# Masked attention followed by an ELU layer: the two products six blocks behind attention, the weight conversion over three engines, the first batch loaded in long pieces

## The chip, the cores and the metric

The kernel runs on one core of a Trainium2 chip, in one launch. The metric is the device time of one execution in microseconds (us); less is better. The time before is the median of three runs, 1208.84 us (1207.19 to 1209.16).

PE is TensorE (PEld its weight loads), ACT ScalarE, DVE VectorE, POOL GpSimd, and SP the engine on whose queue every DMA here is issued (SPq).

## What is computed

The input has 4 batches, 8 heads, 768 tokens and 64 numbers per head. Queries and keys are assigned to one of 16 cluster centroids per head, and a query attends only to keys of its own cluster. The heads are put side by side (512 numbers per token), and two products with an ELU between them follow. `w_in` and `w_out` arrive as 64-bit floats; all else is fp32.

```python
mask = q_assign[:, :, :, None] == k_assign[:, :, None, :]
scores = scale * np.matmul(q, k.transpose(0, 1, 3, 2))
scores = np.where(mask, scores, -1000000000.0)
attn = np.exp(scores - max); attn = attn / (sum(attn) + 1e-9)
x = (attn @ v) with heads side by side        # 3072 x 512
h = x @ w_in                                  # 512 -> 2048
out = where(h > 0, h, exp(min(h, 0)) - 1) @ w_out   # 2048 -> 512
```

## The kernel before

**Blocks.** Two heads make a pair, four pairs a batch, and the 768 queries of a pair are cut into two halves of 384. A pair and a half make a *block*: 8 blocks in a batch, 32 in all, in the order batch, pair, half.

**Attention of a block.** `score` (line 300) does six key tiles. For each, PE multiplies keys by queries for both heads (line 308, fp32, two heads side by side in the array) and adds the mask as a bf16 product of one-hot keys `hot` with `qm` (line 317); ACT takes the exponential into `p` (line 325). `add` (line 328) sums the six `p` for the denominator, on POOL in batch 0 and on DVE afterwards. `values` (line 337) multiplies by `v` into `o_bank`; `divide` (line 350) sums over the keys on PE (line 355), ACT copies that sum out (line 360), DVE takes its reciprocal (line 361), and POOL multiplies the output `xT` by it and keeps a running sum (lines 363 and 364).

**What a batch needs first.** `turn` transposes queries and keys of a pair on PE (line 232; a copy by ACT for queries, by DVE for keys). `similar` multiplies all four pairs by the centroids (line 249) and turns the result by halves on DVE (line 256); `assign` makes the one-hot tile `hot` (lines 263 to 274), `masks` the tile `qm` (line 280). `prepare` gives these steps for the next batch their places beside the current one. Queries and keys are loaded so that both heads of a token lie together, in packets of 256 bytes, two DMAs to a tile.

**The products.** `mlp` (line 367) makes four groups for each half of a batch: two of `hidden` (lines 375 to 388: 16 fp32 products into a bank, exponential on ACT, a clamp on POOL, the ELU's end on DVE one step later) and two of `outer` (lines 401 to 411, into `o_bank` or `f_bank`, then a copy and a DMA out). The groups of batch b run beside the attention of batch b+1, one group after each block. So batch 0 has attention alone, batches 1 to 3 both, and a last pass the eight groups of batch 3 alone.

**Weights.** 32 pieces (16 of `w_in`, then 16 of `w_out`) of 128 x 512 64-bit numbers, 512 KB each, are loaded as pairs of words and made fp32. `convert` (line 176) does this with six instructions on DVE (lines 187 to 199) and two on POOL (lines 188 and 200), each piece in two steps; words have two buffers. `weigh(2)` after every key tile of batch 0 takes two steps from this list. So all conversion lies in the opening and in batch 0.

**What sets the order.** Each engine does its instructions in the order in which the program writes them, and an instruction that waits holds up all behind it on that engine; the DMAs wait on SP in the same way. The score tiles, sums, transposes and hidden products share three PSUM tiles (`banks`) in turn.

Of the kernel before, what the change touches and what calls it, by code (L numbers as in the profile page):

```python
# [9 lines left out]
F32 = mybir.dt.float32  # L10
BF16 = mybir.dt.bfloat16
# [49 lines left out]
def main_path(ctx, tc, c, q, k, v, centroids, moe_w_in, moe_w_out, out):  # L61
# [19 lines left out]
    xtp = ctx.enter_context(tc.tile_pool(name="xtp", bufs=10))  # L81
# [12 lines left out]

    pairs = [(b, pr) for b in range(B) for pr in range(NPR)]
    raw = {}

    def load(name, i):
        b, pr = pairs[i]
        src = {"q": q, "k": k, "v": v}[name]  # L100
        if name == "v":
            t = raw[name, i] = loads.tile([P, 2, NT, D], F32, name="v_raw", tag=name, bufs=2)
# [4 lines left out]
            return  # L107
        t = loads.tile([P, NT, 2, D], F32, name=f"{name}_raw", tag=name, bufs=2)
        for e in range(2):
            nc.sync.dma_start(t[:, :, e], src[b, 2 * pr + e].rearrange("(p t) d -> p t d", t=NT))  # L110
        raw[name, i] = t.rearrange("p t h d -> p t (h d)")
# [3 lines left out]
    for name in "qk":  # L115
        load(name, 0)
    for name in "qk":
        load(name, 1)
# [53 lines left out]

    w_in, w_out = c["w_in"], c["w_out"]
    WC = 512
    wide = moe_w_in.dtype != F32

    def convert(to, src):

        if not wide:
            return [lambda: nc.sync.dma_start(to, src)]  # L180
        words = loads.tile([P, WC, 2], U32, name="words", tag="words", bufs=2)
        ex = loads.tile([P, WC], U32, name="ex", tag="ex", bufs=1)
        low, high, bits = words[:, :, 0], words[:, :, 1], to.bitcast(U32)
        nc.sync.dma_start(words.rearrange("p n w -> p (n w)"), src.bitcast(U32))

        def begin():
            nc.vector.tensor_scalar(bits, high, 0xFFFFF, None, op0=Alu.bitwise_and)
            nc.gpsimd.tensor_scalar(to, bits, 2.0**-20, 1.0, op0=Alu.mult, op1=Alu.add)
            nc.vector.tensor_scalar(  # L189
                ex, high, 20, 0x7FF, op0=Alu.logical_shift_right, op1=Alu.bitwise_and  # L190
            )
            nc.vector.tensor_scalar(ex, ex, -896.0, 0.0, op0=Alu.add, op1=Alu.max)  # L192
            nc.vector.tensor_scalar(ex, ex, 255.0, 2.0**23, op0=Alu.min, op1=Alu.mult)  # L193
            nc.vector.scalar_tensor_tensor(
                ex, high, 0x80000000, ex, op0=Alu.bitwise_and, op1=Alu.bitwise_or
            )

        def end():
            nc.vector.scalar_tensor_tensor(to, low, 2.0**-52, to, op0=Alu.mult, op1=Alu.add)
            nc.gpsimd.tensor_tensor(to, to, ex.bitcast(F32), op=Alu.mult)  # L200

        return [begin, end]

    def weights():
        for g in range(DF // WC):
            for ch in range(KC):
                yield w_in[:, ch, ts(g, WC)], moe_w_in[ts(ch, P), ts(g, WC)]
        for f in range(FC):
            yield w_out[:, f], moe_w_out[ts(f, P)]

    def weight_steps():

        held = None
        for to, src in weights():
            steps = convert(to, src)
            if held:
                yield from held
            held = steps
            yield lambda: None
        yield from held  # L220
# [7 lines left out]
    def turn(i, j):  # L228
        T[i, j] = turned.tile([P, S], F32, name=f"{name_of[j]}T", tag="turned")
        ps = banks()  # L230
        for t in range(NT):
            nc.tensor.transpose(ps[:, t // HT, ts(t % HT, P)], raw[name_of[j], i][:, t], ident)  # L232
        to = T[i, j].rearrange("p (h s) -> p h s", h=2)
        if j == 0:
            nc.scalar.copy(to, ps[:, :, :HS])
        else:
            nc.vector.tensor_copy(to, ps[:, :, :HS])  # L237

    def similar(b, j):
        sim[b, j] = route.tile([P, S], F32, name="sim", tag="sim", bufs=1)  # L240
        ps = banks()
        for half in range(2):
            cols = slice(half * HS, (half + 1) * HS)
            for x in range(2):
                for e in range(2):
                    for g in range(2):
# [5 lines left out]
                            rhs=T[b * NPR + pr, j][:, cols],  # L252
# [3 lines left out]
            nc.vector.transpose(sim[b, j][:, cols], ps[:, half, :HS])  # L256
# [19 lines left out]
    def masks(i):  # L276
        b, pr = pairs[i]
        qm[i] = route.tile([P, S], BF16, name="qm", tag="qm", bufs=2)
        s = big[:, pr : pr + 1]
        nc.vector.tensor_scalar(qm[i], hot[b, 0], s, s, op0=Alu.mult, op1=Alu.subtract)  # L280

    def prepare(b):

        plan = {}
        for pr in range(NPR):
            i = b * NPR + pr
            at = 2 * NT * pr
            for j in range(2):
                plan.setdefault(at + j, []).append(lambda i=i, j=j: turn(i, j))
            if i + 2 < len(pairs):  # L290
                plan[at + 1].append(lambda i=i: (load("q", i + 2), load("k", i + 2)))
        for j in range(2):
            plan.setdefault(6 * NPR * 2 - 10 + 2 * j, []).append(lambda j=j: similar(b, j))
            plan.setdefault(6 * NPR * 2 - 9 + 2 * j, []).append(lambda j=j: assign(b, j))
        plan.setdefault(6 * NPR * 2 - 4, []).append(lambda: masks(b * NPR))
        return plan


    pu, osum, xT = {}, {}, {}

    def score(i, half, kts):
        b, pr = pairs[i]
        cols = slice(half * HS, (half + 1) * HS)
        for kt in kts:
# [10 lines left out]
            for e in range(2):  # L315
# [4 lines left out]
                    rhs=qm[i][rows, cols],  # L320
# [3 lines left out]
            p = pu[i, half, kt] = probs.tile([P, 2, HS], F32, name="p", tag="p")  # L324
            nc.scalar.activation(p, s[:, :, :HS], Act.Exp, scale=SCALE)  # L325

    def add(i, half, kt, eng):
        if kt == 0:
            return
        if kt == 1:  # L330
            osum[i, half] = work.tile([P, 2, HS], F32, name="psum", tag="psum")
        to = osum[i, half]
        eng.tensor_tensor(  # L333
            to, pu[i, half, 0] if kt == 1 else to, pu[i, half, kt], op=Alu.add
        )

    def values(i, half, kt):
        for e in range(2):
            nc.tensor.matmul(  # L339
                o_bank[64 * e : 64 * e + 64, :HS],  # L340
                lhsT=raw["v", i][:, e, kt],
                rhs=pu[i, half, kt][:, e],
                start=(kt == 0),
                stop=(kt == NT - 1),
            )
        if kt == NT - 1:
            x = xT[i, half] = xtp.tile([P, HS], F32, name="xT", tag="xT")
            nc.scalar.copy(x, o_bank[:, :HS])
            divide(i, half)

    def divide(i, half):
        s = osum.pop((i, half))
# [6 lines left out]
        n = 2 * i + half  # L359
        nc.scalar.activation(r, d[:, :HS], Act.Copy, accum_out=d_sum[:, n : n + 1])  # L360
        nc.vector.reciprocal(r, r)  # L361
        x = xT[i, half]
# [4 lines left out]
    def mlp(b, half, last):  # L367
# [51 lines left out]
        for parts in (  # L419
            [(0, 0), (0, 1), (0, 2), (0, 3), (1, 0), (1, 1)],  # L420
# [6 lines left out]


    load("v", 0)
    rest = weight_steps()  # L430

    def weigh(n):
        for _ in range(n):
            step = next(rest, None)
            if step:
                step()

    plan = prepare(0)
    weigh(2)
    for n in sorted(plan):  # L440
        for step in plan[n]:
            step()
        weigh(1)

    units = 2 * NPR * NT
    pending = []

    def flush(left):
        while len(pending) > left:
            values(*pending.pop(0))  # L450

    for b in range(B + 1):
        groups = []
        if b > 0:
            for half in range(2):
                groups.extend(mlp(b - 1, half, b == B))
        plan = prepare(b + 1) if b + 1 < B else {}
        G = NT if b else 1
        assert b == 0 or len(groups) == units // G
        for n in range(0, units, G):  # L460
            if b:
                flush(0)
            if b < B:
                i, half, kt = b * NPR + n // (2 * NT), (n // NT) % 2, n % NT
                kts = range(kt, kt + G)
                within = range(n % (2 * NT), n % (2 * NT) + G)
                if 3 in within and i + 1 < len(pairs):
                    load("v", i + 1)
                score(i, half, kts)
                pending.extend((i, half, x) for x in kts)  # L470
                if 2 * NT - 3 in within and pairs[i][1] + 1 < NPR:
                    masks(i + 1)
                for x in kts:
                    add(i, half, x, nc.vector if b else nc.gpsimd)
            if b == 0:
                flush(2)
                weigh(2)
# [254 lines left out]
```

## Time and profile before

| | |
|---|---|
| median of three runs | 1208.84 us |
| the profiled execution | 1209.18 us |
| its span, first to last instruction | 1207.4 us |
| PE busy | 1078.6 us (89%) |
| DVE / POOL / ACT busy | 499.6 / 284.9 / 268.4 us |
| moved by DMA | 42.7 MB |

The median and the profiled execution differ by 0.34 us. The table's busy times are sums over the whole span; the stages differ much, so the sections below go by stage. Where a row has a granted clock, 1.00 is TensorE at 2.4 GHz all the time, and less means that it ran at 1.2 GHz for a part.

### The profile page before, as it was taken

The numbers are of one execution on the slowest core, as the hardware profiler recorded it, in microseconds if no ns is written. First come the engines' busy times: TensorE is split into PE (matmuls) and PEld (weight loads), VectorE is DVE, ScalarE is ACT, GpSimd is POOL, SyncE is SP. The second block draws the span as 40 slices with busy tenths as digits, with TensorE's granted clock in tenths as the row PEclk, the third lists the DMA queues.
The fourth block names the chain that finished last, engine by engine and source line by source line (L and its number), as shares of the span: only waits on it lengthen the run. The fifth ranks groups of instructions, "written<-read, shape, count | busy, mean of one in ns | idle before, by whom it ended". The sixth has DMA issues, their size and how long they took to land.

```text
span 1207.4 us, 10470 instructions
## 1 busy us (share of the span) xinstructions
PE 1078.6 (89%) x4291; PEld 522.1 (43%) x4291; DVE 499.6 (41%) x516; ACT 268.4 (22%) x395; POOL 284.9 (24%) x239
## 2 busy tenths in 40 slices
PE   5646374388999999999999999999999999999997
PEld 3212121125544555345544554455445544554553
DVE  5788888743432343523422344334323432110110
ACT  1112121122322232223322221223222322110100
POOL 2366666652210121112200111112101111110100
PEclk9778777789999999999999999999999999999999
DMA  9424232300001101001010000000000000000000
GB/s 231 119 70 110 71 110 73 103 1 26 14 24 31 38 14 40 10 31 27 14 35 30 1 14 10 9 23 1 22 10 22 1 10 9 9 0 18 9 9 20
DMA packets 62791, 42.73 MB, mean 35 GB/s; under 512 B 51472, under 2 KB 55568, under 8 KB 62736
## 3 DMA queue, kind: packets, MB, share of 16 engines
q1 hardware_dynamic: 62736, 41.98, 12.6%
q8 instruction: 36, 0.59, 0.2%
q14 instruction: 19, 0.16, 0.0%
HBM read 35.68 MB, written 6.29 MB: 35 GB/s over the span
## 4 chain that ended last, share of the span: by engine, by line
PE 79%; DVE 8%; POOL 7%; issue 3%; DMA 1%; SPq 1%; ACT 0%; POOLq 0%; ACTq 0%
PE banks L375 28%; PE o_bank L401 18%; PE f_bank L401 9%; PE banks L308 9%; PE o_bank L339 9%; POOL psum L333 3%; PE banks L317 2%; PE banks L249 2%; DVE ex L189 2%; POOL w_out L200 1%; PE banks L355 1%; DVE ex L193 1%; DVE r L361 1%; PE banks L232 1%; DVE ex L192 1%
## 5 line engine op out<-in xcount | busy, mean ns | idle before, releaser
L375 PE MATMUL banks<-xT,w_in 128*128 128x384 f32 x1024 | 334.6, 488 | 0.0
L375 PEld LDWEIGHTS banks<-xT,w_in 128*128 128x128 f32 x1024 | 193.5, 190 | 137.4 <-issue 5.9
L401 PE MATMUL o_bank<-w_out,gT 128*128 128x512 f32 x512 | 224.9, 595 | 0.0
L325 ACT ACTIVATE p<-banks 128x768 f32<-128x768 f32 x192 | 153.9, 810 | 148.5 <-PE banks L317 142.4
L361 DVE RECIPROCAL r<-r 128x384 f32<-128x384 f32 x32 | 81.7, 2552 | 250.0 <-ACT r L360 250.0
L308 PE MATMUL banks<-qT,kT 64*128 64x384 f32 x768 | 172.9, 530 | 6.4 <-DVE kT L237 6.4
L388 DVE SCALAR_TENSOR_TENSOR gT<-gT,banks 128x768 f32<-128x768 f32 x64 | 61.1, 954 | 278.8 <-POOL gT L385 278.4
L363 POOL TENSOR_TENSOR xT<-xT,r 128x384 f32<-128x384 f32 x32 | 42.7, 1336 | 454.9 <-DVE r L361 454.9
L401 PEld LDWEIGHTS o_bank<-w_out,gT 128*128 128x128 f32 x512 | 95.9, 190 | 119.1 <-issue 118.6
L339 PE MATMUL o_bank<-p,v_raw 128*64 128x384 f32 x768 | 145.4, 512 | 0.0
L385 POOL TENSOR_SCALAR gT<-gT 128x768 f32<-128x768 f32 x64 | 52.9, 827 | 327.1 <-ACT gT L384 327.1
L333 DVE TENSOR_TENSOR psum<-psum,p 128x768 f32<-128x768 f32 x96 | 114.8, 1196 | 10.4 <-ACT p L325 0.5
L384 ACT ACTIVATE gT<-banks 128x768 f32<-128x768 f32 x64 | 51.8, 810 | 281.1 <-PE banks L375 281.1
L401 PE MATMUL f_bank<-w_out,gT 128*128 128x512 f32 x256 | 112.9, 593 | 0.0
L308 PEld LDWEIGHTS banks<-qT,kT 64*128 64x128 f32 x768 | 67.7, 196 | 81.9 <-issue 65.9
L317 PE MATMUL banks<-qm,hot 64*128 64x384 bf16 x384 | 65.8, 336 | 29.4 <-DVE qm L280 29.4
L339 PEld LDWEIGHTS o_bank<-p,v_raw 128*64 128x64 f32 x768 | 49.9, 140 | 83.2 <-issue 82.5
L401 PEld LDWEIGHTS f_bank<-w_out,gT 128*128 128x128 f32 x256 | 48.4, 190 | 60.5 <-issue 60.5
L355 PE MATMUL banks<-psum,ones 128*64 128x384 f32 x128 | 31.2, 571 | 46.9 <-POOL psum L333 46.9
L333 POOL TENSOR_TENSOR psum<-psum,p 128x768 f32<-128x768 f32 x32 | 58.7, 1834 | 10.3 <-ACT p L325 9.5
L189 DVE TENSOR_SCALAR ex<-words 128x512 uint32<-128x512 uint32 x32 | 43.8, 1368 | 32.3 <-POOL w_out L200 17.6
L410 ACT COPY o_sb<-o_bank 128x512 f32<-128x512 f32 x16 | 9.4, 586 | 207.2 <-PE o_bank L401 207.2
(74 smaller groups left out, 534.9 us busy)
## 6 DMA issues: line engine op xcount, KB each, us to landing
words<-in_moe_w_in_dram SPq DMA_DIRECT2D x16, 512.0 KB, 4.0
words<-in_moe_w_out_dram SPq DMA_DIRECT2D x16, 512.0 KB, 3.5
q_raw<-in_q_dram SPq DMA_DIRECT2D x32, 192.0 KB, 4.2
k_raw<-in_k_dram SPq DMA_DIRECT2D x32, 192.0 KB, 4.2
v_raw<-in_v_dram SPq DMA_DIRECT2D x16, 384.0 KB, 3.2
out_dram<-o_sb SPq DMA_DIRECT2D x24, 256.0 KB, 2.0
cen<-in_centroids_dram SPq DMA_DIRECT2D x1, 32.0 KB, 1.7
```

Source lines behind the costliest of these rows:

```text
L189: nc.vector.tensor_scalar(ex, high, 20, 0x7FF, op0=Alu.logical_shift_right, op1=Alu.bitwise_and)
L308: nc.tensor.matmul(s[:, e, :HS], lhsT=T[i, 1][rows, ts(kt, P)], rhs=T[i, 0][rows, cols], start=True, stop=False,)
L317: nc.tensor.matmul(s[:, e, :HS], lhsT=hot[b, 1][rows, ts(kt, P)], rhs=qm[i][rows, cols], start=False, stop=True,)
L325: nc.scalar.activation(p, s[:, :, :HS], Act.Exp, scale=SCALE)
L333: eng.tensor_tensor(to, pu[i, half, 0] if kt == 1 else to, pu[i, half, kt], op=Alu.add)
L339: nc.tensor.matmul(o_bank[64 * e : 64 * e + 64, :HS], lhsT=raw["v", i][:, e, kt], rhs=pu[i, half, kt][:, e], start=(kt == 0), stop=(kt == ...
L361: nc.vector.reciprocal(r, r)
L375: nc.tensor.matmul(h[:, e, :HS], lhsT=w_in[:, ch, ts(2 * n + e, P)], rhs=xT[b * NPR + ch, half], start=(ch == 0), stop=(ch == KC - 1),)
L384: nc.scalar.activation(t, h[:, :, :HS], Act.Exp)
L385: nc.gpsimd.tensor_scalar(t, t, 1.0, 0.0, op0=Alu.min, op1=Alu.max)
L388: lambda: nc.vector.scalar_tensor_tensor(t, t, -1.0, h[:, :, :HS], op0=Alu.add, op1=Alu.max)
L401: nc.tensor.matmul(o, lhsT=g[f // 2][:, f % 2, ts(t, P)], rhs=w_out[:, f], start=(f == 0), stop=(f == FC - 1),)
```

## The change

- **Order.** Blocks now run batch, half, pair. The product groups stand in one list of 32, and group n-6 follows block n: the first group comes after block 6, and six groups are left when the blocks are done. `values` and the division of block n-1 stand ahead of the scores of block n everywhere. The transposes of the next batch are two at a time at the start of blocks 2, 5, 6 and 7 of a batch. `v` is loaded once per block.
- **First batch.** Its `q`, `k` and `v` come with 1536-byte runs, one DMA to a tile, all eight `q` and `k` tiles at once ahead of everything (four of them in the still unused `w_out` tile). Heads then don't lie together, so `turn` uses two fp32 products with the identity per token tile instead of one transpose, and ACT does all the copies. The weight conversion starts only with block 0.
- **Sums.** In blocks 0 to 5 POOL adds tiles 0 to 2 and DVE tiles 3 to 5 and the part of POOL; later DVE adds all.
- **Conversion.** Per piece DVE has four instructions, ACT two (Identity and Relu), POOL one. A piece n is begun in step n and ended in step n+1. Seven places hold loaded words, five of them in `w_out`; pieces from the 17th on (those of `w_out`) may use only the two places of their own. Two steps are taken in each of blocks 0 to 5, then two after every step of the groups beside blocks 6, 7 and 8.
- **Small.** `similar` does both halves before the DVE turns; `qm` is made for one half; the first outer group ends with `o_bank` instead of `f_bank`; ten `xT` buffers become eight.

```diff
+        if staged:
+            t = take(2 * NT * D)
+        else:
+            t = loads.tile([P, 2 * NT * D], F32, name=f"{name}_raw", tag=name, bufs=2)
+        if name == "v" or b == 0:
+            t = t.rearrange("p (h t d) -> p h t d", h=2, t=NT)
             nc.sync.dma_start(
                 t.rearrange("p h t d -> p h (t d)"),
                 src[b, 2 * pr : 2 * pr + 2].rearrange("h (p t) d -> p h (t d)", t=NT),
             )
...
     for name in "qk":
-        load(name, 0)
-    for name in "qk":
-        load(name, 1)
+        for i in range(NPR):
+            load(name, i, staged=i >= 2)
+    load("v", 0)
...
+    def ask():
...
+            if asked >= into:
+                places[:] = [x for x in places if x[1]]
+            if not places:
+                return
+            place, own = places.pop(0)
+            w = place.bitcast(U32)
+            nc.sync.dma_start(w, src.bitcast(U32))
...
     def weight_steps():
...
+        for n in range(len(pieces) + 1) if wide else ():
+            if n > 0:
...
+                nc.scalar.activation(to, to.bitcast(U32), Act.Identity, scale=2.0**-20, bias=one)
+                nc.scalar.activation(ex, ex, Act.Relu, scale=8.0, bias=off)
+            if n < len(pieces):
+                high = words[n][0][:, :, 1]
...
+                nc.vector.tensor_scalar(
+                    pieces[n][0].bitcast(U32), high, 0xFFFFF, None, op0=Alu.bitwise_and
+                )
+                nc.vector.tensor_scalar(e, high, 0x7FF00000, None, op0=Alu.bitwise_and)
+            if n > 0:
+                w, place, own = words.pop(n - 1)
+                nc.vector.scalar_tensor_tensor(
+                    ex, w[:, :, 1], 0x80000000, ex, op0=Alu.bitwise_and, op1=Alu.bitwise_or
+                )
+                nc.vector.scalar_tensor_tensor(
+                    to, w[:, :, 0], 2.0**-52, to, op0=Alu.mult, op1=Alu.add
+                )
+                nc.gpsimd.tensor_tensor(to, to, ex.bitcast(F32), op=Alu.mult)
+                places.append((place, own))
+                ask()
+            yield
...
+            for e in range(2):
+                nc.tensor.matmul(
+                    to[64 * e : 64 * e + 64], lhsT=src[:, e, t], rhs=ident, start=True, stop=True
+                )
...
+        if shared:
+            part = gtp.tile([P, 2, HS], F32, name="part", tag="gT")
+            nc.gpsimd.tensor_tensor(part, pu[n, 0], pu[n, 1], op=Alu.add)
+            nc.gpsimd.tensor_tensor(part, part, pu[n, 2], op=Alu.add)
+            nc.vector.tensor_tensor(to, pu[n, 3], pu[n, 4], op=Alu.add)
+            nc.vector.tensor_tensor(to, to, pu[n, 5], op=Alu.add)
+            nc.vector.tensor_tensor(to, to, part, op=Alu.add)
...
-            [(0, 0), (0, 1), (0, 2), (0, 3), (1, 0), (1, 1)],
+            [(0, 0), (1, 0), (0, 1), (1, 1), (0, 2), (0, 3)],
...
+    for n in range(len(blocks) + LAG):
+        b, at = n // NB, n % NB
+        ahead = b + 1 < B
+        if ahead and at in turns:
+            for j in range(2):
+                turn((b + 1) * NPR + turns[at], j)
+        if n <= len(blocks) and n > 0:
+            values(n - 1)
...
+        if n < LAG:
+            weigh(1)
+        if n < len(blocks):
+            scores(n)
+            if at + 1 < NB:
+                masks(n + 1)
+            sums(n, n < LAG)
...
+        main = groups[n - LAG] if n >= LAG else []
+        if n < LAG:
+            weigh(1)
+        done = 0
+        for m, step in enumerate(main):
             step()
+            upto = len(beside) * (m + 1) // len(main)
+            for other in beside[done:upto]:
+                other()
+            done = upto
+            if n < LAG + 3:
                 weigh(2)
```

## Rows read from the trace of the kernel before

**Rows 1.** The profile page: the span

```profile
span 1207.4 us, 10470 instructions
```

**Rows 2.** Three stages: length, busy PE, PEld, DVE, ACT, POOL, clock, DMA share, GB/s

```profile
0.00:49.40 49.40, 24.27 (x125) 13.29 (x125) 32.17 (x68) 6.77 (x8) 11.01 (x17) 0.90 0.76 170
49.40:276.30 226.90, 132.63 (x613) 45.46 (x612) 171.19 (x188) 48.71 (x73) 146.07 (x109) 0.77 0.28 83
276.30:1035.50 759.20, 756.38 (x3107) 378.17 (x3105) 277.18 (x235) 195.83 (x290) 112.60 (x96) 1.00 0.06 18
```

**Rows 3.** The chain that ended last, batch 0: start us, us, what

```profile
79.15 2.47 DVE r L361
...
109.13 2.47 DVE r L361
```

**Rows 4.** Timeline, 121 us: start, duration, engine, line

```profile
121.42 1.79 POOL L333 TENSOR_TENSOR psum<-psum,p 128x768 f32<-128x768 f32 x1
121.49 2.01 DVE L189 TENSOR_SCALAR ex<-words 128x512 uint32<-128x512 uint32 x1 [1.15 <-POOL w_in L200]
```

**Rows 5.** Tile words, 150 to 277 us: ns min/median/max; landing time

```profile
L189 DVE TENSOR_SCALAR ex<-words x13: 415/2008/2029, 151.4 to 243.7; 128x512 uint32<-128x512 uint32 x13
L194 DVE SCALAR_TENSOR_TENSOR ex<-words,ex x13: 691/693/693, 156.2 to 245.1; 128x512 uint32<-128x512 uint32 x13
...
DMA to landing us min/median/max: 3.4/3.5/3.7
```

**Rows 6.** Timeline of the opening and of the first mask

```profile
0.75 1.28 ACT L143 ACT_TABLE_LOAD   x1 [0.75 <-PEq L713]
...
5.72 1.51 PE L232 MATMUL banks<-ident,q_raw 128*128 128x128 f32 x6
...
25.81 2.79 PE L249 MATMUL banks<-qT,cTz 128*32 128x384 f32 x16
...
29.30 1.50 PE L249 MATMUL banks<-qT,cTz 128*32 128x384 f32 x16 [0.70 <-DVE sim L256]
...
40.90 0.58 DVE L256 STREAM_TRANSPOSE sim<-banks 128x384 f32<-128x384 f32 x1 [2.91 <-PE banks L249]
...
43.50 0.98 DVE L274 STREAM_TRANSPOSE hot<-oh 128x768 bf16<-128x768 bf16 x1
...
47.51 0.51 PE L317 MATMUL banks<-qm,hot 64*128 64x384 bf16 x2 [5.10 <-DVE qm L280]
```

**Rows 7.** Groups by line, 49 to 277 us: busy us, mean ns, idle before

```profile
L333 POOL TENSOR_TENSOR psum<-psum,p 128x768 f32<-128x768 f32 x32 | 58.7, 1834 | 10.3 <-ACT p L325 9.5
...
L361 DVE RECIPROCAL r<-r 128x384 f32<-128x384 f32 x7 | 17.8, 2547 | 4.6 <-ACT r L360 4.6
L200 POOL TENSOR_TENSOR w_in<-w_in,ex 128x512 f32<-128x512 f32 x12 | 16.4, 1368 | 18.4 <-DVE w_in L199 18.4
...
L363 POOL TENSOR_TENSOR xT<-xT,r 128x384 f32<-128x384 f32 x7 | 8.9, 1277 | 23.3 <-DVE r L361 23.3
L364 POOL TENSOR_TENSOR r_sum<-r_sum,r 128x384 f32<-128x384 f32 x7 | 8.2, 1173 | 0.0
```

**Rows 8.** Line 333 over the span: ns min/median/max

```profile
L333 DVE TENSOR_TENSOR psum<-psum,p x96: 957/959/1573, 281.7 to 1013.6; 128x768 f32<-128x768 f32 x96
```

**Rows 9.** Groups by line, 277 to 1035 us

```profile
L388 DVE SCALAR_TENSOR_TENSOR gT<-gT,banks 128x768 f32<-128x768 f32 x48 | 45.8, 954 | 170.7 <-POOL gT L385 170.2
...
L385 POOL TENSOR_SCALAR gT<-gT 128x768 f32<-128x768 f32 x48 | 39.7, 826 | 219.9 <-ACT gT L384 219.9
...
L410 ACT COPY o_sb<-o_bank 128x512 f32<-128x512 f32 x12 | 7.0, 586 | 141.2 <-PE o_bank L401 141.2
```

**Rows 10.** Timeline, first block of batch 1: scores and six exponentials

```profile
276.34 1.65 PE L308 MATMUL banks<-qT,kT 64*128 64x384 f32 x4
...
278.33 4.85 ACT L325 ACTIVATE p<-banks 128x768 f32<-128x768 f32 x6 [1.24 <-PE banks L317]
```

**Rows 11.** The chain at its end: eight steps of hidden without attention

```profile
1118.22 41.28 PE banks L375 x128
```

More of the change, by code (lines that the diff above doesn't have):

```diff
@@ L96, in main_path, with take, load @@
     raw = {}
[L98 removed]
+    spare = c["w_out"].rearrange("p f m -> p (f m)")
+    used = 0
+    def take(n):
+        nonlocal used
+        used += n
+        return spare[:, used - n : used]
+    def load(name, i, staged=False):
         b, pr = pairs[i]
         src = {"q": q, "k": k, "v": v}[name]
[L101 to L102 removed]
+        if staged:
[4 more added lines that the diff above has]
+            t = t.rearrange("p (h t d) -> p h t d", h=2, t=NT)
             nc.sync.dma_start(
@@ L106, in load @@
             )
[L107 to L111, printed above, removed]
+        else:
+            t = t.rearrange("p (t h d) -> p t h d", t=NT, h=2)
+            for e in range(2):
+                nc.sync.dma_start(
+                    t[:, :, e], src[b, 2 * pr + e].rearrange("(p t) d -> p t d", t=NT)
+                )
+        raw[name, i] = t
     cen, ident = c["cen"], c["ident"]
@@ L175, in main_path @@
     wide = moe_w_in.dtype != F32
[L177 to L209, printed above, removed]
-    def weight_steps():
[L213 to L220, printed above, removed]
+    pieces = [
+        (w_in[:, ch, ts(g, WC)], moe_w_in[ts(ch, P), ts(g, WC)])
+        for g in range(DF // WC)
+        for ch in range(KC)
+    ]
@@ new lines, in main_path @@
+    into = len(pieces)
+    pieces += [(w_out[:, f], moe_w_out[ts(f, P)]) for f in range(FC)]
+    one = const.tile([P, 1], F32, name="one")
+    off = const.tile([P, 1], F32, name="off")
+    nc.gpsimd.memset(one, 1.0)
+    nc.gpsimd.memset(off, -896.0 * 2**23)
+    words, exps = {}, {}
+    places = []
+    asked = 0
+    def ask():
+        nonlocal asked
+        while asked < len(pieces):
+            to, src = pieces[asked]
+            if not wide:
+                nc.sync.dma_start(to, src)
+                asked += 1
+                continue
+            if asked >= into:
[5 more added lines that the diff above has]
+            nc.sync.dma_start(w, src.bitcast(U32))
+            words[asked] = (w.rearrange("p (n w) -> p n w", w=2), place, own)
+            asked += 1
@@ L225, in main_path, with weigh @@
+    for n in range(2):
+        places.append((loads.tile([P, 2 * WC], F32, name="words", tag=f"words{n}"), True))
+    while used + 2 * WC <= FC * DM:
+        places.append((take(2 * WC), False))
+    ask()
+    rest = weight_steps()
+    def weigh(n):
+        for _ in range(n):
+            next(rest, None)
     T, sim, hot, qm = {}, {}, {}, {}
@@ L241, in similar @@
         ps = banks()
-        for half in range(2):
-            cols = slice(half * HS, (half + 1) * HS)
-            for x in range(2):
+        for x in range(2):
+            for half in range(2):
                 for e in range(2):
@@ L255, in similar @@
                         )
-            nc.vector.transpose(sim[b, j][:, cols], ps[:, half, :HS])
+        for half in range(2):
+            nc.vector.transpose(
+                sim[b, j][:, half * HS : (half + 1) * HS], ps[:, half, :HS]
+            )
     def assign(b, j):
@@ L274, in assign, with masks, scores @@
         nc.vector.transpose(hot[b, j], oh)
-    def masks(i):
-        b, pr = pairs[i]
-        qm[i] = route.tile([P, S], BF16, name="qm", tag="qm", bufs=2)
+    def masks(n):
+        b, half, pr = blocks[n]
+        qm[n] = route.tile([P, HS], BF16, name="qm", tag="qm", bufs=2)
         s = big[:, pr : pr + 1]
[L280 to L296, printed above, removed]
+        nc.vector.tensor_scalar(
+            qm[n],
+            hot[b, 0][:, half * HS : (half + 1) * HS],
+            s,
+            s,
+            op0=Alu.mult,
+            op1=Alu.subtract,
+        )
+    blocks = [(b, half, pr) for b in range(B) for half in range(2) for pr in range(NPR)]
     pu, osum, xT = {}, {}, {}
-    def score(i, half, kts):
-        b, pr = pairs[i]
+    def scores(n):
+        b, half, pr = blocks[n]
+        i = b * NPR + pr
         cols = slice(half * HS, (half + 1) * HS)
-        for kt in kts:
+        for kt in range(NT):
             s = banks()
@@ L323, in score @@
                 )
-            p = pu[i, half, kt] = probs.tile([P, 2, HS], F32, name="p", tag="p")
+            p = pu[n, kt] = probs.tile([P, 2, HS], F32, name="p", tag="p")
             nc.scalar.activation(p, s[:, :, :HS], Act.Exp, scale=SCALE)
-    def add(i, half, kt, eng):
-        if kt == 0:
-            return
[L330 to L352, printed above, removed]
+    def sums(n, shared):
+        to = osum[n] = work.tile([P, 2, HS], F32, name="psum", tag="psum")
+        if shared:
[5 more added lines that the diff above has]
+            nc.vector.tensor_tensor(to, to, part, op=Alu.add)
+            return
+        nc.vector.tensor_tensor(to, pu[n, 0], pu[n, 1], op=Alu.add)
+        for kt in range(2, NT):
+            nc.vector.tensor_tensor(to, to, pu[n, kt], op=Alu.add)
@@ new lines, in values @@
+    def values(n):
+        b, half, pr = blocks[n]
+        i = b * NPR + pr
+        for kt in range(NT):
+            for e in range(2):
+                nc.tensor.matmul(
+                    o_bank[64 * e : 64 * e + 64, :HS],
+                    lhsT=raw["v", n][:, e, kt],
+                    rhs=pu[n, kt][:, e],
+                    start=(kt == 0),
+                    stop=(kt == NT - 1),
+                )
+        x = xT[i, half] = xtp.tile([P, HS], F32, name="xT", tag="xT")
+        nc.scalar.copy(x, o_bank[:, :HS])
+        s = osum.pop(n)
@@ L452, in main_path @@
[L452 to L476, printed above, removed]
-                weigh(2)
-            beside = [step for m in range(n, n + G) for step in plan.get(m, [])]
-            main = groups[n // G] if b else []
-            done = 0
-            for m, step in enumerate(main):
-                step()
-                upto = len(beside) * (m + 1) // len(main)
-                for other in beside[done:upto]:
-                    other()
-                done = upto
-            for other in beside[done:]:
-                other()
-            if b == 1:
-                weigh(2 * G)
@@ L491, in main_path, with load_v @@
-    weigh(1000)
+    LAG = 6
+    NB = 2 * NPR
+    turns = {2: 0, 5: 1, 6: 2, 7: 3}
+    groups = [g for b in range(B) for half in range(2) for g in mlp(b, half)]
+    def load_v(n):
+        b, half, pr = blocks[n]
+        if n not in seen:
+            seen.add(n)
+            load("v", b * NPR + pr)
+            raw["v", n] = raw.pop(("v", b * NPR + pr))
+    seen = {0}
+    raw["v", 0] = raw.pop(("v", 0))
+    for j in range(2):
+        for pr in range(NPR):
+            turn(pr, j)
+        similar(0, j)
+        assign(0, j)
@@ L494, in main_path @@
+    weigh(100)
     ok = c["ok"]
```

55 lines of the change are left out of this document (30 added, 25 removed).

## The prediction

> **What bounds the kernel now.** I read the span first, then busy time by stage, because an average of 89% for PE hides where it idles. From 276.3 to 1035.5 us PE is busy 756.4 of 759.2 us at the full clock; before that it is busy 24.3 of 49.4 and then 132.6 of 226.9 us, at clocks of 0.90 and 0.77 [rows 1, 2]. So nearly everything that can be won without less PE work lies in the first 276 us. There the reader should see that DVE and POOL are busy 171.2 and 146.1 us [rows 2].
>
> The chain of waits in that stage goes from one reciprocal to the next in 30.0 us, one block of attention with four weight pieces [rows 3]. Two timeline rows tell why it is long: the mask of line 189 begins 0.07 us after a POOL addition of 1.79 us, and ends 0.29 us after it, having taken 2.01 us instead of its least 0.415 [rows 4, 5]. The DVE addition of line 333 likewise has 957 ns at best and 1573 at worst [rows 8]. I read this as exclusion: such an instruction of DVE and one of POOL do not run side by side, so their durations add up. The stage is bound by that sum, and PE by the stage.
>
> **The change, step by step.** The sum goes in order of time and is made against the profiled execution: 1209.2 us, of which 1207.4 is span and 1.8 lies around it. It stands 0.3 us above the median.
>
> *Opening, to the first mask product: 33 us, where it was 47.5* [rows 6]. The first transpose starts at 5.7 us, after the centroids, and this remains. Four `similar` sets of 384 columns, two in each half, price fp32 products: 2.79 us for two sets at the low level, 1.50 at the high one, hence 0.47 and 0.25 us for the 128 columns of a token tile. A turn of six such tiles is then 2.8 or 1.5 us. I let two turns and nothing else run low, since PE has no gaps there any more: 5.7 + 2 x 2.8 + 2 x 1.5, a copy of 0.9, `similar` 3.0, four turns of keys 6.0, copy 0.9, `similar` 3.0, and on DVE one more turn of 0.58 and the chain from 40.90 to 44.48, then `qm` 0.3: 33. All low it would be 46; no row shows weight loads for such short products, so 46 is the upper end. Data do not set it: eight tiles of 393 KB at the opening's 170 GB/s [rows 2] take 18.5 us, keys are wanted from 18 on.
>
> *Block 0: 12 us, to 45.* Six key tiles of about 1.65 us at first [rows 10], two last additions, the division. An estimate; 9 to 15.
>
> *Blocks 1 to 5: 17.4 us each, to 132.* On DVE two steps, each of two masks at 0.42 and two combinations at 0.69, 4.4 [rows 5], and three additions at 0.96 [rows 8]; on POOL two additions at 1.83, two weight products at 1.37, and 1.28 + 1.17 for the division [rows 7]. By exclusion 7.3 + 8.9 = 16.2. The reciprocal's 2.55 lies beside one POOL product, so 1.2 is left. Were nothing excluded, the dependent chain (reciprocal, two division steps, weight product, two additions, DVE's last addition, a step) is 13.2. I take the first, being nearest to [rows 4].
>
> Rule against this part: the Trainium skill, SBUF — State Buffer, "Who interferes with whom", says that a DVE instruction with two SBUF inputs shuts out a GpSimd one that reads SBUF and that the second to issue fully blocks. By it a sum split between the two engines gains no time side by side, and the sum is 17.4 as above; without it 13.2. [...]
>
> ACT carries two more instructions per step. A copy of 512 columns takes 0.586 [rows 9], so 2.3 us a block beside 4.85 of exponentials [rows 10], hidden below 17.4. In front of the scores they hold up the exponentials queued behind them by 1.2; POOL is later still, so nothing is lost. Unknown is whether Identity and Relu need table loads of 1.28 [rows 6]: none, or two per step. I take none, since copies among exponentials bring none; with two, the step in front of the scores puts 2.6 into each of six blocks, 15 in all.
>
> *Block 6 to the end of piece 14: 27 us, to 159.* Division 2.45 on POOL, five additions 4.8, four steps with their weight product (2.2 + 1.37) 14.3, one ELU end 0.95 and two clamps 0.83 [rows 5, 7 to 9], and the reciprocal. PE could do its block in this time.
>
> *Pieces 16 to 29 under blocks 6 and 7: 96 us.* This is the step that counts against the change. Step n+1 opens with the mask of piece n+1, whose words go where piece n-1 lay; that place is free only when step n ends, since from piece 16 on there are two places. So DVE, in order, stands through a whole load: 3.5 us to landing [rows 5], 0.1 for the hand-overs, 2.2 of work, 5.8 a step. Before, the load of the next piece ran beside the piece at work. Of 14 steps three find their load covered, one by block 7's attention and two by `assign`, and cost 2.2. So 11 x 5.8 + 3 x 2.2 = 70.4; attention of block 7 11 (reciprocal, exponentials, five additions); twice `assign` with an ELU end 10.2; last ELU end and `qm` 1.3. Then ACT must do its part of step 31 before the exponentials of block 8: 3.1 + 2.4, less the 2.0 by which exponentials follow scores [rows 10]. Who waits: PE, through the three `banks`, which the ELU ends behind these steps set free. So the scores of block 8 stand at 159 + 96 = 255, with two groups done. Without any load to wait for, 11 steps cost 3.6 each, 24 us less. Longer: 4.5 us to landing would add 10.
>
> *The rest: 892 us.* Twenty-four blocks follow with their groups, as from 276.34 before: 931.1 to the end of the span. Two of the last eight groups are already done, 41.3 [rows 11]. Added: six times PE wants `o_bank` straight after `outer` and waits for its copy, 0.59 and some 0.2 [rows 9], 4.8 in all; saved: four waits of 0.70 inside `similar` [rows 6]. Net 2.
>
> *Edits at nothing.* Sixteen more loads of `v` on SP, each behind `values` of two blocks earlier, go with a DMA share of 0.06 [rows 2]; uncovered, they would delay `values` a block later. Twice as many half-wide `qm`, turns two at a time, eight `xT` buffers: each is ready a block early. The piece loads queue behind `v` on SP, which at that point waits for nothing.
>
> Sum: 33 + 12 + 87 + 27 + 96 + 892 = 1147, and 1.8 around it: **1149 us**, 5% less.
>
> **Rivals.**
>
> *A, loads hidden* (the words arrive in time, exclusion alone sets the steps): 1149 - 24 = 1125. For it: landing never passes 3.7 us there; against it: nothing else stands on DVE between two steps of a pair.
>
> *B, DVE and POOL overlap*: five blocks at 13.2 and four weight products beside DVE, 21 + 5 less, 1123. Against it [rows 4]; for it, the additions' usual 959 ns [rows 8].
>
> *C, the opening stays at the low level*: 1161. For it: with the engine busy most of the time the six transposes at 5.72 took 1.51 us, and `similar` still began low at 25.81 [rows 6].
>
> *D, ACT loads tables at every change of function*: 1164. The Trainium skill, ScalarE: Activation LUTs, "Table sets: the hidden batching unit", has relu and identity in every set, by which D fails; no run here shows either function.
>
> *E, slower than before: the round trip of the `w_out` pieces.* Its place is steps 16 to 31, its price about 13 times what landing exceeds 3.5 us, less the 3 us that `assign` still covers. It decides where 60 us are lost: at 8.3 us to landing. Against it: the range 3.4 to 3.7 [rows 5]. For it: loads of `v`, queries and keys share the queue, and any other wait that falls between a step's end and the next load is paid in the same way, sixteen times.
>
> **How the numbers follow.** Forecast 0.50, A 0.12, B 0.14, C 0.14, D 0.05, E 0.05. The forecast's own bounds are 1137 (block 0 short, less waiting) to 1165 (blocks at 19, landing 4.5). The range 1114 to 1180 adds A to D with some way beyond; A and B together (1099) and E are outside. About 0.2% is what a measurement of this kernel can tell from no change. All but E end more than that below 1208.8: faster 0.94, same 0.01, slower 0.05.
>
> **What would show it.** The first mask product near 33 us; reciprocals about 17 us apart in blocks 1 to 5; DVE idle some 3.6 us before the masks of pieces 16 to 31, put down to the DMA of the words, eleven times in two blocks; the first score of block 8 near 255 us; PE without gaps after that and 892 us long. Wrong if the reciprocals stand 13 us apart, if no such DMA waits are seen, or if PE has regular gaps after block 8.

## The result and the profile after

The changed kernel takes 1131.4 us (median of four runs, 1128.3 to 1133.2) against 1209.0 of the kernel before on the same chip: a ratio of 0.9355, 95% interval 0.9327 to 0.9384. The forecast was 1149, its range 1114 to 1180. A later repetition gave 1128.3 (ratio 0.9327, 0.9314 to 0.9340). The profile below is of an execution of 1133.2 us, 1131.4 of it span; that this span equals the median is chance.

The page of the changed kernel, with the span [rows 1], the busy times, and PE and its clock in 40 slices (28.3 us each):

```profile
span 1131.4 us, 10777 instructions
PE 1055.9 (93%) x4435; PEld 530.9 (47%) x4435; DVE 449.1 (40%) x492; ACT 311.4 (28%) x463; POOL 226.2 (20%) x181
PE   7878857759999999999999999999999999999997
PEclk9888888969999999999999999999999999999999
```

PE lost 23 us of busy time and the span 76: most of what went was idle time of PE. What idleness is left lies in the first nine slices. By stages (columns as in [rows 2]): opening, blocks 0 to 5, block 6 to the end of piece 14, pieces 16 to 31, then the stretch bound by PE:

```profile
0.00:28.90 28.90, 19.96 (x263) 15.35 (x265) 11.83 (x34) 9.16 (x11) 1.13 (x9) 0.98 0.86 293
28.90:121.00 92.10, 74.44 (x422) 34.96 (x421) 74.76 (x79) 50.65 (x80) 52.84 (x33) 0.87 0.39 103
121.00:147.00 26.00, 25.87 (x89) 14.69 (x90) 18.12 (x26) 13.41 (x19) 9.03 (x8) 0.89 0.00 1
147.00:240.30 93.30, 55.02 (x251) 26.28 (x249) 53.35 (x88) 30.99 (x49) 28.25 (x24) 0.79 0.28 89
240.30:1041.40 801.10, 797.71 (x3189) 397.41 (x3190) 282.11 (x254) 198.34 (x294) 128.31 (x101) 1.00 0.10 27
```

Timeline rows of PE that answer to [rows 6]: turns of two tiles, the first mask product, and (for [rows 10]) the first score of block 8:

```profile
5.73 5.25 PE L279 MATMUL banks<-ident,q_raw 128*64 128x128 f32 x48
10.81 2.79 PE L279 MATMUL banks<-ident,w_out 128*64 128x128 f32 x48
13.53 2.79 PE L297 MATMUL banks<-qT,cTz 128*32 128x384 f32 x32
...
28.86 0.50 PE L362 MATMUL banks<-qm,hot 64*128 64x384 bf16 x2 [3.58 <-DVE qm L331]
...
240.31 1.65 PE L353 MATMUL banks<-qT,kT 64*128 64x384 f32 x4 [2.63 <-ACT r L408]
```

One of blocks 1 to 5, from reciprocal to reciprocal, in timeline rows (rows of PE weight loads, of ACT's exponentials and of the second step are left out):

```profile
57.41 2.54 DVE L409 RECIPROCAL r<-r 128x384 f32<-128x384 f32 x1
...
60.03 1.05 POOL L410 TENSOR_TENSOR xT<-xT,r 128x384 f32<-128x384 f32 x1 [2.06 <-DVE r L409]
60.15 1.21 DVE L237 TENSOR_SCALAR ex<-w_out 128x512 uint32<-128x512 uint32 x1
61.04 1.17 POOL L411 TENSOR_TENSOR r_sum<-r_sum,r 128x384 f32<-128x384 f32 x1
61.28 1.48 DVE L240 SCALAR_TENSOR_TENSOR ex<-w_out,ex 128x512 uint32<-128x512 uint32 x1
...
63.45 1.36 POOL L246 TENSOR_TENSOR w_in<-w_in,ex 128x512 f32<-128x512 f32 x1 [1.23 <-DVE w_in L243]
63.58 2.03 DVE L379 TENSOR_TENSOR psum<-p 128x768 f32<-128x768 f32 x1
...
64.76 2.52 POOL L377 TENSOR_TENSOR part<-p 128x768 f32<-128x768 f32 x1
...
65.72 2.38 DVE L380 TENSOR_TENSOR psum<-psum,p 128x768 f32<-128x768 f32 x1
...
67.36 2.40 POOL L378 TENSOR_TENSOR part<-part,p 128x768 f32<-128x768 f32 x1
69.79 0.96 DVE L381 TENSOR_TENSOR psum<-psum,part 128x768 f32<-128x768 f32 x1 [1.69 <-POOL part L378]
...
70.89 1.55 PE L404 MATMUL banks<-psum,ones 128*64 128x384 f32 x4 [4.42 <-DVE psum L381]
...
72.70 1.27 POOL L246 TENSOR_TENSOR w_in<-w_in,ex 128x512 f32<-128x512 f32 x1 [2.94 <-DVE w_in L243]
...
73.15 2.55 DVE L409 RECIPROCAL r<-r 128x384 f32<-128x384 f32 x1 [0.53 <-ACT r L408]
```

Follow the additions. The DVE one at 63.58 starts while POOL's weight product runs to 64.81 and takes 2.03 us where 0.96 is its least; POOL's at 64.76 then waits for it and takes 2.52 where 1.80 is its least [rows 4]; the next DVE one 2.38, the next POOL one 2.40. Each takes its own time and the rest of the neighbour's, less 0.13 to 0.16 us. DVE's last addition, at 69.79, starts when POOL is done and takes 0.96. The reciprocal takes 2.55 with a weight product beside it (72.70) as without one (81.04 in the run with all sums on POOL, below).

A step of the `w_out` pieces, DVE's timeline, and below it the sum of such waits from 147 to 240 us:

```profile
150.61 0.43 DVE L234 TENSOR_SCALAR w_out<-words 128x512 uint32<-128x512 uint32 x1 [2.74 <-DMA words<-in_moe_w_out_dram]
150.95 0.42 DVE L237 TENSOR_SCALAR ex<-words 128x512 uint32<-128x512 uint32 x1
151.29 0.68 DVE L240 SCALAR_TENSOR_TENSOR ex<-words,ex 128x512 uint32<-128x512 uint32 x1
151.89 0.68 DVE L243 SCALAR_TENSOR_TENSOR w_in<-words,w_in 128x512 f32<-128x512 uint32 x1
156.08 0.43 DVE L234 TENSOR_SCALAR w_out<-words 128x512 uint32<-128x512 uint32 x1 [3.51 <-DMA words<-in_moe_w_out_dram]
```

```profile
DVE w_out L234 <- DMA words<-in_moe_w_out_dram: 38.2, 12, 3.6
```

DVE stands 38.2 us in twelve waits there, and PE is busy 55 of 93.3 us.

### The profile page after: what moved, and what is told of

It is laid out like the page before. It is cut to its first block, busy times and chain, and to the rows that moved or that the text cites. A ratio compares the mean times of both kernels' runs of the same rounds, so it can differ in the third digit from the quotient of the medians.

```text
span 1131.4 us, 10777 instructions
## 1 busy us (share of the span) xinstructions
PE 1055.9 (93%) x4435; PEld 530.9 (47%) x4435; DVE 449.1 (40%) x492; ACT 311.4 (28%) x463; POOL 226.2 (20%) x181
## 4 chain that ended last, share of the span: by engine, by line
PE 83%; DVE 7%; DMA 4%; POOL 3%; ACT 2%; issue 1%; ACTq 0%; POOLq 0%; DVEq 0%
PE banks L422 26%; PE o_bank L448 20%; PE banks L353 10%; PE f_bank L448 10%; PE o_bank L392 9%; DMA words<-in_moe_w_out_dram 4%; PE banks L362 2%; PE banks L404 2%; PE banks L297 1%; PE banks L279 1%; POOL part L377 1%; DVE ex L240 1%; POOL part L378 1%; ACT p L370 1%; PE banks L275 1%; POOL w_in L246 1%
## 5 line engine op out<-in xcount | busy, mean ns | idle before, releaser
L410 POOL TENSOR_TENSOR xT<-xT,r 128x384 f32<-128x384 f32 x32 | 52.3, 1633 | 424.4 <-DVE r L409 424.4
L392 PE MATMUL o_bank<-p,v_raw 128*64 128x384 f32 x768 | 132.8, 496 | 2.7 <-ACT o_sb L457 2.7
L385 DVE TENSOR_TENSOR psum<-psum,p 128x768 f32<-128x768 f32 x104 | 130.6, 1256 | 11.8 <-DVE psum L385 0.9
L353 PEld LDWEIGHTS banks<-qT,kT 64*128 64x128 f32 x768 | 73.3, 205 | 71.0 <-issue 43.2
L392 PEld LDWEIGHTS o_bank<-p,v_raw 128*64 128x64 f32 x768 | 52.8, 138 | 76.0 <-issue 68.9
L286 DVE COPY kT<-banks 128x768 f32<-128x768 f32 x12 | 11.4, 954 | 104.4 <-PE banks L275 104.4
L411 POOL TENSOR_TENSOR r_sum<-r_sum,r 128x384 f32<-128x384 f32 x32 | 51.3, 1604 | 0.0
```

The source lines that it names most:

```text
L353: nc.tensor.matmul(s[:, e, :HS], lhsT=T[i, 1][rows, ts(kt, P)], rhs=T[i, 0][rows, cols], start=True, stop=False,)
L385: nc.vector.tensor_tensor(to, to, pu[n, kt], op=Alu.add)
L392: nc.tensor.matmul(o_bank[64 * e : 64 * e + 64, :HS], lhsT=raw["v", n][:, e, kt], rhs=pu[n, kt][:, e], start=(kt == 0), stop=(kt == NT - 1),)
L410: nc.gpsimd.tensor_tensor(x, x, r, op=Alu.mult)
```

## Experiments

The kernel before took 1209.4, 1209.8 and 1209.8 us in the three sets of runs, so ratios compare across them. The changed kernel itself gave 1131.4 and 1128.3, so what an edit gains or costs is known to some 3 us; where one figure stands below, it is against 1131.4. Each edit is on the changed kernel.

**Words earlier, in two ways.** First the step's end ahead of its beginning, so that the load is asked for before the mask that waits:

```diff
-            if n < len(pieces):
-                ...
             if n > 0:
                 ...
                 ask()
+            if n < len(pieces):
+                ...
```

> One edit on the changed kernel: within a conversion step the end of piece n-1 stands ahead of the beginning of piece n, so a place is free a whole step before its next words are wanted. Theory (the round trip of the words through two places sets steps 16 to 31, 5.6 us each): a step falls to the landing time or to its own work with the wait for ACT, about 3.7 us; DVE's waits for the DMA of the words (41.8 us in 13) fall below 10 us; the first score of block 8 comes at 220 instead of 240 us and the time is 1111 +- 6. Rival (DVE and POOL work is the bound there, the wait for words is only what is left over): 1127 to 1133.

Measured 1122.1 us, ratio 0.9278 (0.9264 to 0.9293), 9.3 us less: under half of the 20 expected. Waits for words are 0.5 us in one. What came in their place, in DVE's waits from 130 to 230 us:

```profile
DVE ex L233 <- ACT ex L230: 14.7, 12, 3.7
```

The combination now stands straight behind ACT's Identity and Relu (0.71 us each), which before ran while DVE did the next masks. In blocks 1 to 5 the order costs as well: reciprocals 16.65 us apart instead of 15.92. The second way keeps the order and adds a place (its memory taken from an output buffer):

```diff
-    for n in range(2):
+    for n in range(3):
...
-                o_sb = work.tile([P, DM], F32, name="o_sb", tag="o_sb")
+                o_sb = work.tile([P, DM], F32, name="o_sb", tag="o_sb", bufs=1)
```

> The order of the changed kernel, but a third place for words (paid for with one output buffer fewer), so that the load of a piece starts one step earlier. Theory (round trip through two places): the same gain as with the swapped order, DVE's waits for words below 10 us, first score of block 8 near 220, time 1111 +- 6. Rival (the loads themselves are slow when they follow each other, whatever the place): DVE still waits some 3 us at every step, 1128 to 1133.

Measured 1102.9 us, ratio 0.9113 (0.9099 to 0.9127), 28.5 us less (25.4 against the repetition): more than expected. Waits for words and the first score of block 8:

```profile
DVE w_out L234 <- DMA words<-in_moe_w_out_dram: 1.0, 3, 0.4
```

```profile
213.61 1.65 PE L353 MATMUL banks<-qT,kT 64*128 64x384 f32 x4 [0.45 <-ACT r L408]
```

That score comes 26.7 us earlier, while the waits for words had been 38.2 us. What took the place of the rest is mostly POOL's weight product, which now falls beside DVE's masks. From 147.0 us to that score DVE's waits add up to 8.0 us, most of them for these products, and its busy time is 57.2 us instead of 53.4, with masks of up to 1.50 us instead of 0.42:

```profile
DVE ex L237 <- POOL w_out L246: 4.6, 4, 1.2
DVE ex L237 <- POOL w_in L246: 1.2, 1, 1.2
```

```profile
163.07 1.27 POOL L246 TENSOR_TENSOR w_out<-w_out,ex 128x512 f32<-128x512 f32 x1 [1.96 <-DVE w_out L243]
163.13 1.50 DVE L234 TENSOR_SCALAR w_out<-words 128x512 uint32<-128x512 uint32 x1 [0.19 <-DMA words<-in_moe_w_out_dram]
```

So the loads had hidden part of the exclusion, which is the next limit of this stage.

**The sum split between POOL and DVE.** All additions of blocks 0 to 5 on DVE, or all on POOL:

```diff
-            sums(n, n < LAG)
+            sums(n, False)
```

> In blocks 0 to 5 DVE does all five additions, POOL none. Theory (DVE and POOL shut each other out, so that splitting the sum gains only what the order leaves): per block 3.6 us of POOL additions go and 1.9 of DVE additions come; reciprocals 14 to 16.5 us apart instead of 15.9; time 1122 to 1135. Rival (they run side by side and the split halves the sum): POOL is then idle and DVE alone carries 3.9 + 4.8 + 2.55 and the hand-overs, with the additions no longer covered: 18 us or more a block, 1142 and above.

Measured 1124.3 us, ratio 0.9285 (0.9271 to 0.9300), reciprocals 14.9 apart: as expected. The split costs 4 to 7 us.

```diff
-            nc.gpsimd.tensor_tensor(part, part, pu[n, 2], op=Alu.add)
-            nc.vector.tensor_tensor(to, pu[n, 3], pu[n, 4], op=Alu.add)
-            nc.vector.tensor_tensor(to, to, pu[n, 5], op=Alu.add)
-            nc.vector.tensor_tensor(to, to, part, op=Alu.add)
+            for m in range(2, 5):
+                nc.gpsimd.tensor_tensor(part, part, pu[n, m], op=Alu.add)
+            nc.gpsimd.tensor_tensor(to, part, pu[n, 5], op=Alu.add)
```

> In blocks 0 to 5 POOL makes all five additions of a sum and DVE none. Theory (DVE and POOL shut each other out, a block is the sum of both): three additions move from 0.96 us on DVE to 1.80 us on POOL, so a block grows by 3 x 0.84 = 2.5 us from 15.9 to 18.4, and the time by some 12 to 15 us, to 1140 to 1148 us. By the slope of the run in which DVE made all the sums (two additions moved, 1.0 us less) it would be 17.4 us a block and 1137 to 1141 us. Rival (the two engines mostly overlap and a block is the chain through ACT, DVE and POOL): POOL's own work is 5 x 1.80 + 2 x 1.25 + 2 x 1.0 = 13.5 us, under 15.9, so the blocks stay within 16.4 us and the time below 1136 us.

Measured 1151.4 us, ratio 0.9526 (0.9509 to 0.9542). The rival falls, and the theory's size was too small: a block is 19.94 us, 4.0 more instead of 2.5. In its timeline:

```profile
70.55 6.28 POOL L379 TENSOR_TENSOR part<-part,p 128x768 f32<-128x768 f32 x3
70.68 2.29 DVE L240 SCALAR_TENSOR_TENSOR ex<-w_out,ex 128x512 uint32<-128x512 uint32 x1
...
76.91 1.80 POOL L380 TENSOR_TENSOR psum<-part,p 128x768 f32<-128x768 f32 x1
...
81.04 2.55 DVE L408 RECIPROCAL r<-r 128x384 f32<-128x384 f32 x1 [5.86 <-ACT r L407]
```

DVE stands idle 5.86 us here, so the block is no longer a plain sum of both engines. It is the dependent chain from reciprocal to reciprocal: POOL's additions, then PE's product over keys and ACT's copy, 2.3 us in which neither engine adds. With the split, DVE's second step fills that time (from 70.67 on) and a weight product lies beside the reciprocal; here the step runs beside POOL's additions, the product in the 2.3 us, and beside the reciprocal nothing is left.

**The old conversion in the new order.** Six instructions on DVE and two on POOL, none on ACT:

```diff
-                nc.scalar.activation(to, to.bitcast(U32), Act.Identity, scale=2.0**-20, bias=one)
-                nc.scalar.activation(ex, ex, Act.Relu, scale=8.0, bias=off)
...
-                nc.vector.tensor_scalar(e, high, 0x7FF00000, None, op0=Alu.bitwise_and)
+                nc.gpsimd.tensor_scalar(
+                    pieces[n][0], pieces[n][0].bitcast(U32), 2.0**-20, 1.0, op0=Alu.mult, op1=Alu.add
+                )
+                nc.vector.tensor_scalar(
+                    e, high, 20, 0x7FF, op0=Alu.logical_shift_right, op1=Alu.bitwise_and
+                )
+                nc.vector.tensor_scalar(e, e, -896.0, 0.0, op0=Alu.add, op1=Alu.max)
+                nc.vector.tensor_scalar(e, e, 255.0, 2.0**23, op0=Alu.min, op1=Alu.mult)
```

> The conversion of the kernel before (six instructions on DVE, two on POOL, none on ACT) in the order and places of the changed one. Theory (instructions of DVE and POOL add up): 1.1 us of DVE and 0.7 of POOL more a step, in 30 steps ahead of block 8, reciprocals of blocks 1 to 5 some 3.6 us further apart, time 1172 to 1190. Rival (POOL's part lies beside DVE): reciprocals 2.2 us further apart and 1155 to 1166. Rival (the steps are hidden by the loads of words and by PE): below 1145.

Measured 1155.0 us, ratio 0.9550 (0.9533 to 0.9567), the rival's lower edge; reciprocals 17.95 apart. So the new split is worth 24 to 27 us. Of the 2.0 us that a block is longer, DVE's two extra instructions in each of two steps, 0.34 from start to start, make 1.4 by estimate. POOL's instruction costs less than it lasts:

```profile
62.92 0.68 POOL L235 TENSOR_SCALAR w_in<-w_in 128x512 f32<-128x512 uint32 x1
63.16 0.72 DVE L242 TENSOR_SCALAR ex<-ex 128x512 uint32<-128x512 uint32 x1
```

The DVE one starts with 0.44 us of POOL's still to run and takes 0.72 instead of 0.43. That is the rule of the additions again (0.43 and 0.44, less 0.15); POOL's first 0.24 us stood beside the end of the DVE instruction before, so a step pays 0.3 and not 0.7.

**The lag of the products.** Eight blocks instead of six (and a buffer more for `xT`):

```diff
-    LAG = 6
+    LAG = 8
```

> The products eight blocks behind attention instead of six (and nine xT buffers). Theory (until the last piece of w_out is made, DVE and the loads of words set the time and not PE, so two groups that start two blocks later cost PE little): the first score of block 10 comes near 267 us, 872 us follow, time 1133 to 1149. Rival (the six blocks are what gained, two groups of 20.6 us each): 1165 to 1175.

Measured 1142.1 us, ratio 0.9438 (0.9421 to 0.9455): the theory holds. The first score of block 10 stands at 272.4 us and 869 follow. Two blocks more of attention alone cost 11 to 14 us, not the 41 of two groups. No run brings back the old order of blocks and products, so what that part of the change gained is not measured by itself.

**The opening.** The first batch in 256-byte packets and with one transpose per token tile, still all eight tiles at once:

```diff
-        if name == "v" or b == 0:
+        if name == "v":
...
-            if i >= NPR:
-                nc.tensor.transpose(to, src[:, t].rearrange("p h d -> p (h d)"), ident)
-                continue
-
-            for e in range(2):
-                nc.tensor.matmul(
-                    to[64 * e : 64 * e + 64], lhsT=src[:, e, t], rhs=ident, start=True, stop=True
-                )
+            nc.tensor.transpose(to, src[:, t].rearrange("p h d -> p (h d)"), ident)
```

> On the changed kernel the first batch's q and k are loaded in packets of 256 bytes again, two DMAs to a tile, all eight tiles ahead of everything, and transposed instead of multiplied; ACT still copies. Theory (PE's own work and not the data sets the opening, and what brought most of its 19 us was to keep the weight steps out of it): q turns follow the data and end near 12.6 us, both similar steps run low or half low, first mask product at 32 to 36 us instead of 28.9, time 1134 to 1139. Rival (the long pieces brought the opening): the last k comes after 20 us and the mask product at 40 us or later, 1142 and above.

Measured 1126.0 us, ratio 0.9303 (0.9283 to 0.9323): both missed. The first mask product stands at 27.00 us, 1.9 earlier than with long pieces. Keys then need no long turns:

```profile
12.79 3.91 PE L290 MATMUL banks<-qT,cTz 128*32 128x384 f32 x32
16.63 1.53 PE L274 MATMUL banks<-ident,k_raw 128*128 128x128 f32 x12
18.00 1.47 PE L274 MATMUL banks<-ident,w_out 128*128 128x128 f32 x12
```

Two turns take 1.5 us here and 2.8 with products. So long pieces and products brought nothing; what of the opening's gain is left lies in the rest of the change there (all tiles asked for at once, no weight steps between, the order of `similar`), which these runs don't separate.

**The first outer group** in its old order:

```diff
-            [(0, 0), (1, 0), (0, 1), (1, 1), (0, 2), (0, 3)],
+            [(0, 0), (0, 1), (0, 2), (0, 3), (1, 0), (1, 1)],
```

> The first outer group ends with f_bank again, as in the kernel before. Theory: the six gaps of 0.66 to 0.71 us behind the last product of that group (at 267.5, 523.4, 779.2, 902.1, 1019.9 and 1103.3 us) go, 4 us, and nothing comes in their place: 1127.4. Rival (the last pieces of w_out come too late for that order in block 8, or PE only waits elsewhere): 1131 or more.

Measured 1123.6 us, ratio 0.9290 (0.9278 to 0.9303), 5 to 8 us less. The gap is seen in the chain of the changed kernel, six times, from 0.66 to 0.71 us:

```profile
267.55 0.59 ACT o_sb L457
...
268.19 4.09 PE o_bank L392 x24
```

From the first score of block 8 to the end it is 885.1 us instead of 891.1; six such gaps are 4.1 of these 6.0, about 1.1 more are the scores of block 8 themselves (5.2 instead of 6.3 us, at a granted clock of 0.65 instead of 0.53), and 0.8 is not traced.

**What gained, together**: third place, sums on DVE, old outer order.

> Three edits together on the changed kernel: a third place for words (with one output buffer fewer), all six sums on DVE everywhere, the first outer group ending with f_bank. Theory (they act in three different stretches: steps 16 to 31, blocks 1 to 5, and the time after block 8): their gains add, 28 + 7 + 7, time 1085 to 1094, reciprocals 15 us apart, no waits for words, no gaps behind the outer group. Rival (with the words in time, DVE alone is the bound and the sums moved to it in blocks 0 to 5 push the steps later): 1097 or more.

Measured 1090.8 us, ratio 0.9023 (0.9001 to 0.9045), as expected: the gains add up. Then the short opening on top:

> The three edits that gained (third place for words, all sums on DVE, the old order of the first outer group) with the opening of the kernel before (256-byte packets, two DMAs to a tile, transposes) but still all eight tiles at once. If the short opening is worth on this base what it was worth alone (1126.0 against 1131.4), 1083 to 1088 us; if the 1.9 us at the first mask product are all of it, 1087 to 1091; if the gain was an accident of the order of the loads, 1091 or more.

Measured 1089.5 us, ratio 0.9011 (0.8991 to 0.9032): not to be told from the last. Both beat the two kernels compared, the changed one by 3.3 to 3.6%.

## Why the prediction was right

Its sum was 33 + 12 + 87 + 27 + 96 + 892; the trace has 28.9 + 12.5 + 79.6 + 26.0 + 93.3 + 891.1 (limits: first mask product, reciprocals at 41.38 and 120.99, end of piece 14 at 147.0, first score of block 8 at 240.31, end). The direction and the mechanisms that carry the sum (exclusion, the round trip of the words, PE after block 8) were right, and all terms but block 0 came out under their size; the opening and blocks 1 to 5 carry 11.5 of the 15.8 us between the forecast and the profiled execution.

- **Blocks 1 to 5, 17.4 us each, measured 15.92.** This step was mis-sized by 7.4 in all. POOL's prices came from means in the contended stage of before, which already hold waiting for the other engine, and then the waiting was added again; DVE's were durations, of which each overlaps the next by some 0.08 us. From start to start a step takes 0.34 + 0.34 + 0.60 + 0.60 us (150.61 to 151.89, the last taken like the third), two steps 3.8 and not 4.4; the weight product 1.27, the two division steps 1.01 and about 1.0, an addition 1.80. So 6.7 + 8.2, and 1.3 of the reciprocal, give 16.2. The exclusion itself is seen in all but the last addition of the block shown. The forecast also left out the 2.3 us of PE's product and ACT's copy; they cost nothing as long as DVE's second step lies in them, and the run with all sums on POOL shows their cost without that.
- **Opening, 33, measured 28.9.** Two turns took 5.25 us and the next two 2.79, as put, though the granted clock reads 1.00 from 5.7 us on, so it is open whether the level of the clock makes the first two long. The price itself has the same gap: in the trace before, `similar` at 25.81 took 2.79 at a granted clock of 1.00, and only the one at 38.04, 2.79 as well, at 0.50; so the row that the prediction calls low, for the price and for rival C, does not show the low level. The rest is `similar`, 2.8 instead of 3.0, whose order left no waits of 0.9 for copies. Rival C (no short turns) did not happen.
- **Pieces 16 to 31, 96, measured 93.3.** DVE waits 38.2 us in twelve waits, against eleven of 3.6. Rival A's mechanism, loads hidden, was absent; made true by a third place, it gave 25 to 28 us where 24 stood.
- **Rival B** priced a block at 13.2; neither the trace nor moving additions either way comes to it. **Rival D**: the only table loads are the two of the opening; Identity and Relu take 0.71 us. By the Trainium skill, ScalarE: Activation LUTs, "Table sets: the hidden batching unit", both are in every set, and the trace agrees. ACT's order did cost once: DVE waits 4.6 us for a Relu that stands behind an exponential (at 135.7).
- **Block 6 to the end of piece 14, 27, measured 26.0.** The fit is partly luck: the sum had no such wait of 4.6, and its four steps, put at 14.3, took about 11 without it (130.28 to 146.92, less the wait and an ELU end).
- **Rival E**, slower: landing 3.4 to 4.2 us, far from 8.3.
- **The rest, 892, measured 891.1.** The `o_bank` copy was put at 4.8 and is 4.1 by its gaps.

The rule weighed against the split sum (the Trainium skill, SBUF — State Buffer, "Who interferes with whom") agrees: the later of the two waits for the end of the other (2.03 is 0.96 and the 1.23 that POOL's product still ran, less 0.16), and splitting the sum loses 4 to 7 us against DVE alone.

## What to carry to other kernels

Price an instruction in a contended stage by its least or from start to start, then add the waiting once. When a load goes where the last piece lay, compare its round trip with what the engine still has to do: one more place was worth 25 to 28 us, and reordering the step instead only a third of that, because of a new wait for ACT. Two-input additions split between DVE and POOL gain nothing; give the second engine work that lies beside a reciprocal.

## What was not expected

- Exclusion does not need two inputs. DVE's `TENSOR_SCALAR` with one input is lengthened beside POOL's two-input work (1.21 us at 60.15, least 0.42), as the mask in [rows 4] was; the reciprocal never is (2.53 to 2.56).
- A one-input `TENSOR_SCALAR` of POOL holds up DVE's in the same way: 0.72 for 0.43 with the old conversion, and 1.04 for 0.42 in the changed kernel (at 141.63, beside line 432 from 141.39 to 142.39).
- Packets of 256 bytes were no slower for the opening than runs of 1536: first mask product at 27.00 against 28.86 us, with six transposes in 1.51 us at first and 0.8 later.
- The first fp32 products of the opening took twice what the same ones took 5 us later (5.25 and 2.79 us for 48), at a granted clock of 1.00 in both stretches.
